# A fixed matmul order for the attention stage of a fused attention and two-layer-expert kernel

## The chip, the core and the metric

The kernel runs on one core of one Trainium2 chip. The metric is the device time of one execution in microseconds (us). Before the change three executions took 887.31, 887.38 and 888.92 us, median 887.38 us. The execution that the profiler recorded took 888.05 us.

## The reference

Three parts follow one another; the output of each is the input of the next.

```python
scores = scale * np.matmul(q, k.transpose(0, 1, 3, 2)) - np.log(S)   # q, k, v: 4 x 12 x 448 x 64
attn = 1.0 / (1.0 + np.exp(-scores))
x = np.matmul(attn, v)                                               # 48 heads
...
h = np.maximum(np.maximum(x @ w1, x @ w2), x @ w3)                   # 1792 x 768, weights 768 x 768
x = h @ w_out
...
h = x @ w_in                                                         # 768 x 2048
g = h * (1.0 / (1.0 + np.exp(-1.702 * h)))
out = g @ w_out
```

The attention weights come from a sigmoid and not from a softmax, so each block of scores can be weighed as soon as its own sigmoid is done. This case is about the first part.

## The kernel before

**The planner.** The program does not issue instructions while it describes the work. Every step is an `Op` with the engine or engines that can do it, an estimated length, a function that issues its instructions, and the memory it reads and writes. `Order.op` derives from the memory which earlier steps an `Op` must come after. `Order.run` then walks a simulated time and, for each engine, takes the ready step with the earliest due time (`late`). So the order of each engine's instructions is fixed when the program is built, and is the planner's. On the chip each engine runs its own list in order and waits on semaphores. For steps of TensorE, `Order.pe` keeps a running clock of the estimated lengths and gives every step that clock as its due time; another step's due time is worked back from those that need its result.

**The attention stage.** The 48 heads are worked on as 24 couples of two heads (`Couple`), and the couples in 12 cycles of two: x (even) and y (odd). The 448 keys of a head are 3 blocks of 128 and a last one of 64. For a couple there are these steps on TensorE:

- `score(c)`, line 581, for c = 0, 1, 2: scores of 128 keys against 448 queries. Queries and keys are split into a high and a low part, so three products of each head are summed: 6 matmuls, contraction 64, output 128 rows. The two heads lie in the two halves of the rows of TensorE's array. The result takes a pair of PSUM banks. There are three such pairs, used in turn.
- `score_last`, line 625: the last 64 keys of both couples of a cycle at once, four 64 by 64 matmuls in fp32.
- `weigh(c)`, line 599: the values times the sigmoids of a block, contraction 128, output 64 rows for each head: 2 matmuls in fp32, summed in a bank of the couple's own (6 for x, 7 for y).
- `weigh_last`, line 636: the same for the last 64 keys of both couples, four 64 by 64 matmuls.

The profile records an fp32 matmul as two instructions: a `weigh` is x4, `weigh_last` and `score_last` are x8, a `score` is x6. The three steps use the array in three shapes, which the profile writes as 64*128 (scores), 128*64 (weighing) and 64*64 (the last keys).

ScalarE takes each `score` from PSUM through a sigmoid (line 608), which also frees the pair of banks. ScalarE or VectorE copies a couple's finished bank out (line 307). The queries and keys of a couple are loaded (`in_qk`), split on VectorE with or without ScalarE (lines 307 and 310) into one of two slots, and the values are loaded (`in_vv`) into one of three slots. Beside that, `convert` prepares weights of the next stage, which come as 64-bit numbers: a load of 768 KB (`in_wa`), one instruction on ScalarE (line 355), four on VectorE (lines 365 to 370) and a store (`yk<-f`), two of these in each of cycles 1 to 9. All DMAs are issued by SyncE from one queue (SP), in order.

**The order before.** The loop lists, for cycle i: scores of x; the three `weigh` of the former y; `weigh_last` of the former cycle; `score_last`; scores of y; the three `weigh` of x. The listing only gives due times. The planner takes whichever ready step of TensorE is due first, and it moved `weigh` steps in between the scores.

Of the kernel before, what the change touches and what calls it, by code (L numbers as in the profile page):

```python
# [17 lines left out]
B, H, S, D = 4, 12, 448, 64  # L18
# [4 lines left out]
NPAIR = H // 2  # L23
# [4 lines left out]
HK = KC // 2  # L28
# [14 lines left out]
MM, FULL = 0.201, 0.752  # L43
# [44 lines left out]
class Order:  # L88


    def __init__(self):
        self.ops, self.clock = [], 0.0

    def op(self, on, fn, reads=(), writes=(), after=(), at=None, lag=None):
        lag = (LAND if "SP" in on else 0.1) if lag is None else lag
# [21 lines left out]
        return o  # L117

    def pe(self, fn, took, reads=(), writes=(), after=()):
        o = self.op({"PE": took}, fn, reads, writes, after, self.clock, 0.25)  # L120
        self.clock += took
        return o

    def run(self):
# [60 lines left out]
T = S  # L185
# [18 lines left out]
def moe_chain_kernel(tc, qk, vv, wa, wb, out):  # L204
    nc = tc.nc
    act, dve, pe, sp = nc.scalar, nc.vector, nc.tensor, nc.sync
    scale = 1.0 / math.sqrt(D)
    O = Order()
# [13 lines left out]
    psum = pspool.tile([P, 8, 512], F32, name="ps")  # L222
# [22 lines left out]
    def F(at, n):  # L245
        if at >= FAR2:
            return Reg(sn4, at - FAR2, n, lambda: slab_n[3][:, at - FAR2 : at - FAR2 + n])
        if at >= FAR:
            return Reg(sn1, at - FAR, n, lambda: slab_n[0][:, at - FAR : at - FAR + n])
        return Reg(sf, at, n, lambda: slab_f[:, at : at + n])  # L250
# [52 lines left out]
    def copy(to, of, n, psum=False, both=True):  # L303
        engines = {"ACT": t_act(n)}
        if both:
            engines["DVE"] = t_two(n) if psum else t_one(n)
        return O.op(engines, lambda e: (act.copy if e == "ACT" else dve.tensor_copy)(to(), of()), [of], [to])  # L307
# [15 lines left out]
    XA, XB = 0, FAR  # L323
# [223 lines left out]
    class Couple:  # L547
# [42 lines left out]
            self.a[c] = sigmoid(self.sc[c])  # L590

        def weigh(self, c):
            ps, v = self.av, self.v

            def f(_):
                w, o, x = v().rearrange("p (c d) -> p c d", d=D), ps(), self.a[c]()
                for e in range(2):
                    r = slice(e * D, (e + 1) * D)
                    pe.matmul(o[r], w[:, 2 * c + e], x[:, e * S : (e + 1) * S], start=c == 0, stop=False)  # L599

            O.pe(f, FULL + (0 if c else 0.15), [v, self.a[c]] + ([ps] if c else []), [ps])

    def sigmoid(ps):
        a = M1(a_at(), 2 * S)
        on(
            "ACT",
            t_act(2 * S) + 0.07,
            lambda: act.activation(  # L608
                a().rearrange("p (e s) -> p e s", e=2), ps(), AF.Sigmoid, bias=bias, scale=scale
            ),  # L610
            [ps],
            [a],
        )
        return a

    def score_last(two):

        ps = banks(d_at(), 2)

        def f(_):  # L620
            o = ps()
            for c, x in enumerate(two):
                for e in range(2):
                    r, t = slice(e * D, (e + 1) * D), x.t()
                    pe.matmul(o[c * D : (c + 1) * D, e, :], t[r, QK:QT], t[r, Q:QK], start=True, stop=True)

        O.pe(f, FULL, [x.t for x in two], [ps])
        return ps

    def weigh_last(two, a):  # L630
        def f(_):
            x = a()
            for c, y in enumerate(two):
                w, o, k = y.v().rearrange("p (c d) -> p c d", d=D), y.av(), slice(c * D, (c + 1) * D)
                for e in range(2):
                    pe.matmul(
                        o[e * D : (e + 1) * D], w[k, 6 + e], x[k, e * S : (e + 1) * S], start=False, stop=True
                    )

        O.pe(f, FULL + 0.15, [a, *(y.v for y in two), *(y.av for y in two)], [y.av for y in two])  # L640
        for y in two:
            b, hp = divmod(y.p, NPAIR)
            half, j = divmod(hp, HK)
            copy(F((XA if b < 2 else XB) + (6 * half + 3 * (b % 2) + j) * T, S), y.av, S, psum=True)

# [29 lines left out]
    prev, last = None, None  # L677
    for i in range(NP // 2):
        x = Couple(2 * i)
        x.values()  # L680
        if i == 0:
            x.score(0, slice(0, 1))
            x.score(1, slice(0, 1))
            x.score(0, slice(1, 3))
            x.scored(0)
            x.score(1, slice(1, 3))
            x.scored(1)
        for n in range(0 if i else 2, 3):
            x.score(n)
            x.scored(n)  # L690
        convert(x)
        for n in range(3 if prev else 0):
            prev[1].weigh(n)
        if prev:
            weigh_last(prev, last)
        y = Couple(2 * i + 1)
        y.values()
        last = sigmoid(score_last((x, y)))
        for n in range(3):
            y.score(n)  # L700
            y.scored(n)
        convert(y)
        for n in range(3):
            x.weigh(n)
        prev = (x, y)
    for n in range(3):
        prev[1].weigh(n)
    weigh_last(prev, last)
    gate["m"] = O.op({"-": 0.0}, to_m2, after=set(s1.ops))

    def pairs(base, half, tok, k):
# [48 lines left out]
    x = moving(XA)  # L760
# [3 lines left out]
    x = moving(XB)  # L764
    extra = []
    for fp in range(EARLY):
        for n in range(2):
            extra.append(lambda fp=fp, n=n: prepare(12 + fp, n, "ACT"))
        if fp < READY:
            w = []  # L770
# [99 lines left out]
    half = PAIRS // 2  # L870
# [144 lines left out]
    for n in range(7):  # L1015
# [22 lines left out]
        w = operand4(w)  # L1038
# [85 lines left out]
```

## Time and profile before

| | before |
|---|---|
| median of 3 runs | 887.38 us |
| the profiled execution | 888.05 us |
| its span, first to last instruction | 886.0 us |
| TensorE matmuls busy | 872.7 us (98%) |
| VectorE busy | 685.2 us (77%) |
| ScalarE busy | 504.2 us (57%) |
| DMA queue's packets, share of 16 engines | 75.7% |
| granted TensorE clock | 1.00 throughout, the upper of its two levels (2.4 GHz) |

The profiled execution is 2.05 us longer than its span, which lies around the span and is the same for both kernels. A matmul's recorded length overlaps the next one's, so lengths of steps on TensorE are read here from one group's start to the next group's start.

### The profile page before, as it was taken

How to read it: one execution, taken by the hardware profiler on the slowest of the kernel's cores; microseconds unless marked ns; L12 is line 12 of the kernel's file. 1: busy time of each engine (PE TensorE's matmuls, PEld its weight loads, DVE VectorE, ACT ScalarE, POOL GpSimd, SP SyncE). 2: the span in 40 equal slices, each digit the busy share in tenths (PEclk: the TensorE clock that was granted, in tenths of full speed). 3: DMA queues.
4: the chain of work that ended last, by engine and by line, in shares of the span. 5: the costliest groups of instructions: out<-in, count | busy, mean ns of one | idle time of the engine just before them, and what ended most of it. 6: DMA issues, size and time to landing. Idle time of an engine off the chain costs nothing.

```text
span 886.0 us, 12594 instructions
## 1 busy us (share of the span) xinstructions
PE 872.7 (98%) x4558; PEld 743.6 (84%) x4558; DVE 685.2 (77%) x1100; ACT 504.2 (57%) x738; POOL 1.1 (0%) x6
## 2 busy tenths in 40 slices
PE   9999999999999999999999999999999999999998
PEld 5444447999988987999988999999999999999997
DVE  5787878888899876778598888655778878863894
ACT  6888788455575745567476444556664544423540
POOL 0000000000000000000000000000000000000000
PEclk9999999999999999999999999999999999999999
DMA  7898977676749989879998965999867775686113
GB/s 271 287 343 287 318 275 238 209 251 240 280 196 337 394 285 359 257 260 319 355 410 329 383 212 154 376 367 334 302 244 282 267 258 153 203 286 209 32 63 125
DMA packets 77533, 238.13 MB, mean 269 GB/s; under 512 B 8608, under 2 KB 18208, under 8 KB 77472
## 3 DMA queue, kind: packets, MB, share of 16 engines
q1 hardware_dynamic: 77472, 237.34, 75.7%
q8 instruction: 36, 0.59, 0.3%
q14 instruction: 25, 0.20, 0.1%
HBM read 151.19 MB, written 86.11 MB: 268 GB/s over the span
## 4 chain that ended last, share of the span: by engine, by line
PE 64%; DVE 5%; DMA 3%; ACT 1%; issue 0%; DVEq 0%; SPq 0%; ACTq 0%
PE ps L490 38%; PE ps L851 7%; PE ps L850 7%; PE ps L852 7%; PE ps L992 6%; DVE f L310 2%; DMA r<-kept 2%; DVE r L310 2%; DMA kept<-r 1%; DMA yk<-f 1%; DVE m L310 0%; ACT f L360 0%; DVE f L370 0%; ACT r L307 0%; DVE n L310 0%
## 5 line engine op out<-in xcount | busy, mean ns | idle before, releaser
L490 PE MATMUL ps<-r 128*128 128x448 f32 x2250 | 466.8, 363 | 5.6 <-DVE f L310 2.4
L490 PEld LDWEIGHTS ps<-r 128*128 128x128 f32 x2250 | 421.1, 188 | 38.3 <-DVE r L310 2.2
L310 DVE TENSOR_TENSOR f<-ps,f 128x448 f32<-128x448 f32 x214 | 132.4, 622 | 88.3 <-PE ps L852 35.5
L310 DVE TENSOR_TENSOR r<-f,r 128x384 fp32r<-128x384 f32 (+3 forms) x252 | 160.2, 659 | 14.9 <-ACT r L307 14.2
L307 ACT CAST r<-f 128x384 fp32r<-128x384 f32 (+3 forms) x206 | 111.7, 571 | 65.5 <-PE ps L490 27.0
L307 ACT COPY f<-ps 128x448 f32<-128x448 f32 x130 | 69.7, 542 | 109.5 <-PE ps L490 71.5
L310 DVE TENSOR_TENSOR f<-f 128x384 f32<-128x384 f32 (+2 forms) x189 | 121.1, 658 | 7.6 <-ACT f L913 4.1
L608 ACT ACTIVATE m<-ps,bias 128x896 f32<-128x896 f32 x84 | 80.3, 1009 | 11.7 <-PE ps L581 10.5
L360 ACT ACTIVATE f<-f 128x768 uint8<-128x768 uint32 x38 | 74.9, 1970 | 0.6
L581 PEld LDWEIGHTS ps<-r 64*128 64x128 f32 x432 | 37.2, 185 | 34.2 <-ACT m L608 24.5
L355 ACT ACTIVATE f<-f 128x768 f32<-128x768 f32 x56 | 50.8, 910 | 23.6 <-DMA f<-in_wb 11.7
L599 PE MATMUL ps<-m,f 128*64 128x448 f32 x288 | 63.8, 555 | 0.0
L490 PE MATMUL ps<-m,r 128*128 128x448 f32 x270 | 58.9, 364 | 1.5 <-DVE r L307 0.7
L370 DVE SCALAR_TENSOR_TENSOR f<-f 128x768 uint32<-128x768 uint32 x56 | 53.2, 954 | 5.2 <-ACT f L360 4.6
L581 PE MATMUL ps<-r 64*128 64x448 f32 x432 | 56.4, 385 | 0.3 <-ACT m L608 0.2
L490 PEld LDWEIGHTS ps<-m,r 128*128 128x128 f32 x270 | 50.2, 188 | 6.6 <-DVE r L310 1.3
L365 DVE TENSOR_SCALAR f<-f 128x768 f32<-128x768 f32 x56 | 31.1, 555 | 18.5 <-ACT f L355 18.5
L307 ACT COPY ps<-ps 128x448 f32<-128x448 f32 x43 | 23.3, 542 | 34.9 <-PE ps L490 31.8
L307 ACT CAST m<-f 128x448 fp32r<-128x448 f32 (+4 forms) x36 | 26.1, 724 | 24.4 <-DVE f L310 16.4
L310 DVE TENSOR_TENSOR n<-f,n 128x448 fp32r<-128x448 f32 (+4 forms) x51 | 37.9, 745 | 2.0 <-ACT n L307 1.4
L599 PEld LDWEIGHTS ps<-m,f 128*64 128x64 f32 x288 | 16.7, 135 | 26.4 <-issue 22.8
L310 DVE TENSOR_TENSOR m<-f,m 128x448 fp32r<-128x448 f32 (+4 forms) x41 | 33.9, 831 | 4.0 <-ACT m L307 4.0
(81 smaller groups left out, 892.6 us busy)
## 6 DMA issues: line engine op xcount, KB each, us to landing
r<-kept SPq DMA_DIRECT2D x119, 384.0 KB, 5.2
kept<-r SPq DMA_DIRECT2D x112, 384.0 KB, 5.0
f<-in_wb SPq DMA_DIRECT2D x32, 768.0 KB, 7.2
f<-in_wa SPq DMA_DIRECT2D x24, 768.0 KB, 7.3
f<-yk SPq DMA_DIRECT2D x24, 768.0 KB, 6.0
yk<-f SPq DMA_DIRECT2D x40, 384.0 KB, 7.4
f<-y SPq DMA_DIRECT2D x24, 384.0 KB, 5.2
f<-in_qk SPq DMA_DIRECT2D x15, 456.0 KB, 5.8
```

The costliest lines, as they stand in the source:

```text
L307: return O.op(engines, lambda e: (act.copy if e == "ACT" else dve.tensor_copy)(to(), of()), [of], [to])
L310: return on("DVE", t_two(n), lambda: dve.tensor_tensor(to(), a(), b(), op=op), [a, b], [to])
L360: act.activation(byte(), words(raw(), U32, 0), AF.Copy, scale=LOW)
L370: lambda: dve.scalar_tensor_tensor(u(), words(raw(), U32, 1), 0x80000007, u(), **by),
L490: pe.matmul(o, a[:, c], b, start=fresh and j == n == 0, stop=j == HK - 1 and n == 2, skip_group_check=True,)
L581: pe.matmul(o[:, e, :], kx[r, c * P : (c + 1) * P], qx[r, Q:QK], start=n == 0, stop=n == 2)
L599: pe.matmul(o[r], w[:, 2 * c + e], x[:, e * S : (e + 1) * S], start=c == 0, stop=False)
L608: lambda: act.activation(a().rearrange("p (e s) -> p e s", e=2), ps(), AF.Sigmoid, bias=bias, scale=scale),
L850: pe.matmul(ps(), wh[:, c], gh, start=fresh and j == 0, **how)
L851: pe.matmul(ps(), wh[:, c], gl, start=False, **how)
L852: pe.matmul(ps(), wl[:, c], gh, start=False, stop=j == 1, skip_group_check=True)
L992: pe.matmul(o, a, b, start=fresh and k == n == 0, stop=k == 3 and n == 2, skip_group_check=True)
```

## The change

Every step of TensorE in the attention stage now also comes after the step listed before it (`self.row` in `Order.pe`), so the listed order is the order of TensorE; after the stage this is switched off. The listed order is changed: `weigh_last` of the former cycle and `score_last` follow the scores of x, and the three `weigh` of the former y come after them. `weigh_last` thereby becomes the first addend of y's bank and stays the last of x's, and y's bank is copied out (`give`) after its third `weigh` instead of after `weigh_last`.

```diff
@@ Order
-        self.ops, self.clock = [], 0.0
+        self.ops, self.clock, self.rows, self.row = [], 0.0, True, []
...
     def pe(self, fn, took, reads=(), writes=(), after=()):
-        o = self.op({"PE": took}, fn, reads, writes, after, self.clock, 0.25)
+        o = self.op({"PE": took}, fn, reads, writes, [*after, *self.row], self.clock, 0.25)
         self.clock += took
+        if self.rows:
+            self.row = [o]
         return o
@@ Couple.weigh
-            ps, v = self.av, self.v
+            ps, v, second = self.av, self.v, self.p % 2 == 1
+            begin, end = c == 0 and not second, c == 2 and second
...
-                    pe.matmul(o[r], w[:, 2 * c + e], x[:, e * S : (e + 1) * S], start=c == 0, stop=False)
-
-            O.pe(f, FULL + (0 if c else 0.15), [v, self.a[c]] + ([ps] if c else []), [ps])
+                    pe.matmul(o[r], w[:, 2 * c + e], x[:, e * S : (e + 1) * S], start=begin, stop=end)
+
+            O.pe(f, FULL + (0 if c else 0.15), [v, self.a[c]] + ([] if begin else [ps]), [ps])
+            if end:
+                self.give()
@@ weigh_last
-                        o[e * D : (e + 1) * D], w[k, 6 + e], x[k, e * S : (e + 1) * S], start=False, stop=True
+                        o[e * D : (e + 1) * D], w[k, 6 + e], x[k, e * S : (e + 1) * S], start=c == 1, stop=c == 0
...
-        for y in two:
...
-            copy(F((XA if b < 2 else XB) + (6 * half + 3 * (b % 2) + j) * T, S), y.av, S, psum=True)
+        two[0].give()
@@ the loop over cycles
         convert(x)
-        for n in range(3 if prev else 0):
-            prev[1].weigh(n)
         if prev:
             weigh_last(prev, last)
         y = Couple(2 * i + 1)
         y.values()
         last = sigmoid(score_last((x, y)))
+        for n in range(3 if prev else 0):
+            prev[1].weigh(n)
         for n in range(3):
             y.score(n)
...
+    weigh_last(prev, last)
     for n in range(3):
         prev[1].weigh(n)
-    weigh_last(prev, last)
+    O.rows, O.row = False, []
```

The new lines move the line numbers: scores 581 to 583, `weigh` 599 to 602, the sigmoid 608 to 618, `score_last` 625 to 635, `weigh_last` 636 to 646, the next stage's matmul 490 to 492.

TensorE, one cycle before (581 scores, 599 weighing, 636 `weigh_last`, 625 `score_last`):

```order
L581 MATMUL ps<-r 128x448 x12
L599 MATMUL ps<-m_76,f 64x448 x2
L581 MATMUL ps<-r 128x448 x6
L599 MATMUL ps<-m_76,f 64x448 x4
L581 MATMUL ps<-r 128x448 x12
L599 MATMUL ps<-m_76,f 64x448 x2
L581 MATMUL ps<-r 128x448 x6
L599 MATMUL ps<-m_76,f 64x448 x4
L636 MATMUL ps<-m_76,f 64x448 x4
L625 MATMUL ps<-f 64x448 x4
```

and one cycle now (583 scores, 602 weighing, 646 `weigh_last`, 635 `score_last`):

```order
L583 MATMUL ps<-r 128x448 x18
L646 MATMUL ps<-m_76,f 64x448 x4
L635 MATMUL ps<-f 64x448 x4
L602 MATMUL ps<-m_76,f 64x448 x6
L583 MATMUL ps<-r 128x448 x18
L602 MATMUL ps<-m_76,f 64x448 x6
```

The same matmuls stand in two unbroken groups of scores and two of weighing, where there were four of each.

SyncE's queue, the loads of one cycle before (with what each waits for):

```order
L298 DMA f<-in_vv 128x512 [waits DMAHW3_49,PE_49]
L298 DMA f<-in_vv 128x512 [waits DMAHW4_49,PE_49]
L298 DMA n_77<-in_qk 128x912 [waits DMAHW5_49,PE_49]
L298 DMA f<-in_qk 128x912 [waits DMAHW6_49,DVE_49,PE_49]
L351 DMA f<-in_wa 128x768 [waits DMAHW7_49,DVE_49,Activation_49]
L292 DMA yk_436<-f 128x768 [waits DMAHW0_49]
```

and now:

```order
L300 DMA f<-in_vv 128x512 [waits DMAHW3_49,PE_49]
L300 DMA n_77<-in_qk 128x912 [waits DMAHW4_49,PE_49]
L300 DMA f<-in_qk 128x912 [waits DMAHW5_49,DVE_49,PE_49]
L300 DMA f<-in_vv 128x512 [waits DMAHW6_49,PE_49]
L353 DMA f<-in_wa 128x768 [waits DMAHW7_49,DVE_49,Activation_49]
L294 DMA yk_445<-f 128x768 [waits DMAHW0_49]
```

One of the two loads of values moved behind the loads of queries and keys; nothing else in the cycle's queue did.

SyncE's queue at the start of the program, before (the first couple's queries and keys come in three pieces, 512, 256 and 144 wide):

```order
L298 DMA f<-in_qk 128x512
L298 DMA f<-in_qk 128x256
L298 DMA f<-in_qk 128x144
L298 DMA f<-in_qk 128x912
L298 DMA f<-in_vv 128x512
```

and now:

```order
L300 DMA f<-in_qk 128x512
L300 DMA f<-in_qk 128x256
L300 DMA f<-in_qk 128x912
L300 DMA f<-in_qk 128x144
L300 DMA f<-in_vv 128x512
```

The second couple's load of 456 KB moved ahead of the first couple's third piece of 72 KB.

## Rows read from the trace of the kernel before

**Rows 1.** Waits of TensorE, 0 to 135 us: us in total, times, longest.
```profile
PE ps L581 <- ACT m L608: 0.2, 1, 0.2
```

**Rows 2.** Windows of 10 us: busy us per engine, clock, DMA share, GB/s.
```profile
50.00:60.00 10.00, 10.00 (x72) 4.49 (x70) 9.69 (x15) 7.92 (x11) 0.00 (x0) 1.00 0.99 350
...
260.00:270.00 10.00, 8.84 (x41) 7.52 (x42) 10.00 (x17) 5.18 (x11) 0.00 (x0) 1.00 0.55 219
...
320.00:330.00 10.00, 8.46 (x42) 7.59 (x41) 8.10 (x17) 6.46 (x11) 0.00 (x0) 1.00 0.93 317
...
340.00:350.00 10.00, 9.01 (x44) 7.86 (x43) 6.05 (x12) 6.87 (x7) 0.00 (x0) 1.00 1.02 414
```

**Rows 3.** Timeline of TensorE, one cycle: start us, length us, engine, line, shape.
```profile
64.78 1.48 PE L581 MATMUL ps<-r 64*128 64x448 f32 x12
66.19 0.97 PE L599 MATMUL ps<-m,f 128*64 128x448 f32 x4
67.09 0.87 PE L581 MATMUL ps<-r 64*128 64x448 f32 x6
67.89 1.72 PE L599 MATMUL ps<-m,f 128*64 128x448 f32 x8
69.55 1.49 PE L581 MATMUL ps<-r 64*128 64x448 f32 x12
...
74.33 0.98 PE L636 MATMUL ps<-m,f 64*64 64x448 f32 x8
75.13 0.93 PE L625 MATMUL ps<-f 64*64 64x448 f32 x8
75.99 1.48 PE L581 MATMUL ps<-r 64*128 64x448 f32 x12
```

**Rows 4.** Timeline of TensorE, start and end of the attention stage.
```profile
5.42 2.08 PE L581 MATMUL ps<-r 64*128 64x448 f32 x18
7.43 0.98 PE L625 MATMUL ps<-f 64*64 64x448 f32 x8
8.65 2.67 PE L581 MATMUL ps<-r 64*128 64x448 f32 x18 [0.24 <-ACT m L608]
11.35 2.48 PE L599 MATMUL ps<-m,f 128*64 128x448 f32 x12
13.76 1.48 PE L581 MATMUL ps<-r 64*128 64x448 f32 x12
...
24.70 1.48 PE L581 MATMUL ps<-r 64*128 64x448 f32 x12
...
125.61 1.49 PE L581 MATMUL ps<-r 64*128 64x448 f32 x12
...
139.99 0.47 PE L490 MATMUL ps<-r 128*128 128x448 f32 x1
```

**Rows 5.** Timeline of ScalarE, first pieces of queries and keys.
```profile
5.33 0.31 ACT L307 CAST r<-f 128x144 fp32r<-128x144 f32 x1 [1.31 <-DMA f<-in_qk]
6.79 0.90 ACT L307 CAST r<-f 128x848 fp32r<-128x848 f32 x1 [1.15 <-DMA f<-in_qk]
```

**Rows 6.** DMA issues from 20 to 130 us: KB each, median us to landing.
```profile
f<-in_wa SPq DMA_DIRECT2D x15, 768.0 KB, 8.1
yk<-f SPq DMA_DIRECT2D x17, 384.0 KB, 7.6
f<-in_qk SPq DMA_DIRECT2D x12, 456.0 KB, 6.2
f<-in_vv SPq DMA_DIRECT2D x19, 256.0 KB, 3.2
```

**Rows 7.** Timeline of ScalarE in the cycle of rows 3.
```profile
65.00 2.81 ACT L608 ACTIVATE m<-ps,bias 128x896 f32<-128x896 f32 x3
68.07 1.01 ACT L608 ACTIVATE m<-ps,bias 128x896 f32<-128x896 f32 x1 [0.26 <-PE ps L581]
68.97 0.90 ACT L355 ACTIVATE f<-f 128x768 f32<-128x768 f32 x1
```

More of the change, by code (lines that the diff above doesn't have):

```diff
@@ L598, in f, with give @@
                     r = slice(e * D, (e + 1) * D)
-                    pe.matmul(o[r], w[:, 2 * c + e], x[:, e * S : (e + 1) * S], start=c == 0, stop=False)
-            O.pe(f, FULL + (0 if c else 0.15), [v, self.a[c]] + ([ps] if c else []), [ps])
+                    pe.matmul(o[r], w[:, 2 * c + e], x[:, e * S : (e + 1) * S], start=begin, stop=end)
+            O.pe(f, FULL + (0 if c else 0.15), [v, self.a[c]] + ([] if begin else [ps]), [ps])
+            if end:
+                self.give()
+        def give(self):
+            b, hp = divmod(self.p, NPAIR)
+            half, j = divmod(hp, HK)
+            copy(F((XA if b < 2 else XB) + (6 * half + 3 * (b % 2) + j) * T, S), self.av, S, psum=True)
     def sigmoid(ps):
@@ L636, in f @@
                     pe.matmul(
-                        o[e * D : (e + 1) * D], w[k, 6 + e], x[k, e * S : (e + 1) * S], start=False, stop=True
+                        o[e * D : (e + 1) * D], w[k, 6 + e], x[k, e * S : (e + 1) * S], start=c == 1, stop=c == 0
                     )
-        O.pe(f, FULL + 0.15, [a, *(y.v for y in two), *(y.av for y in two)], [y.av for y in two])
-        for y in two:
-            b, hp = divmod(y.p, NPAIR)
-            half, j = divmod(hp, HK)
-            copy(F((XA if b < 2 else XB) + (6 * half + 3 * (b % 2) + j) * T, S), y.av, S, psum=True)
+        O.pe(f, FULL + 0.15, [a, two[0].av, *(y.v for y in two)], [y.av for y in two])
+        two[0].give()
     warm = R(0, 2 * T)
```

## The prediction

> **What bounds the kernel now.** I read the waits of TensorE first, then the windows, then TensorE's timeline through one cycle.
>
> In the attention stage TensorE waits once, for 0.2 us, after its warm-up matmuls [rows 1]. A window inside the stage shows it busy 10.00 of 10 us, while VectorE at 9.69 us and the DMAs at a share of 0.99 are nearly full as well [rows 2]. So the stage lasts as long as TensorE's own work, and a wait removed elsewhere would bring nothing; the other engines have little room left.
>
> The timeline shows that this work is not only matmuls [rows 3]. From start to start, 12 score matmuls take 66.19 - 64.78 = 1.41 us and 6 take 67.89 - 67.09 = 0.80 us. One block of scores is therefore 0.61 us, and 0.20 us are paid once per group, whatever its size. A `weigh` of 4 takes 67.09 - 66.19 = 0.90 us and 8 take 69.55 - 67.89 = 1.66 us: 0.76 us each and 0.15 us once per group. Each time the array's shape changes, the stream loses 0.15 to 0.20 us. Here it also holds for long groups: 18 scores take 7.43 - 5.42 = 2.01 us = 3 x 0.605 + 0.20, and 12 `weigh` matmuls 13.76 - 11.35 = 2.41 us = 3 x 0.755 + 0.15 [rows 4].
>
> Behind attention TensorE is short of work only in places, in the windows at 260, 320 and 340 us [rows 2]; over the whole span it idles 886.0 - 872.7 = 13.3 us.
>
> **The change, part by part.**
>
> *Fewer groups.* A cycle before is 75.99 - 64.78 = 11.21 us [rows 3], and from cycle 2 to cycle 10 each is as long: (125.61 - 24.70) / 9 = 11.21 us [rows 4]. A cycle now is scores of x (2.01), `weigh_last` (75.13 - 74.33 = 0.80), `score_last` (75.99 - 75.13 = 0.86), three `weigh` (2.41), scores of y (2.01), three `weigh` (2.41): 10.50 us. One passage of it the trace does not have: `score_last` followed by `weigh`. Before, scores followed, at 0.86 us. From below I bound it by 0.80, a 64*64 group followed by one of its own shape; from above by 0.76 + 0.20 = 0.96, a group with the dearest change of shape. I take 0.86, the same group with another change of shape behind it. A cycle then lasts 10.44 to 10.60 us and saves 0.71 us (0.61 to 0.77).
>
> *Eleven cycles and the tail.* Cycle 1 begins at 13.76 us, and the next stage's first matmul at 139.99 us [rows 4]. Now: 13.76 + 11 x 10.50 = 129.26 us, then `weigh_last` alone (0.86, a change of shape behind it) and the last three `weigh` (2.41): 132.53 us. The saving is 139.99 - 132.53 = **7.46 us**, 6.3 to 8.1 us with the bounds above taken eleven times.
>
> *The start.* The load of 456 KB moves ahead of the piece of 72 KB. Before, the small piece had landed by 5.33 us and the large one by 6.79 us [rows 5]; exchanged, the small piece is late by up to 6.79 - 5.33 = 1.46 us, and the large one some 0.2 us early. The third block of scores needs the small piece and would have started at about 5.42 + 1.41 = 6.83 us. Cast and subtraction of that piece take about 0.3 us each, which would put it at 7.1 to 7.4 us: 0.3 to 0.6 us late. Against that, ScalarE is through with the large piece's cast earlier, begins the sigmoids earlier, and y's first scores, which stretched to 11.35 - 8.65 = 2.70 us instead of 2.01 behind those sigmoids [rows 4], gain up to 0.7 us. I take 0, with -0.6 to +0.6.
>
> *The planner's new answer for the other engines.* The sigmoids, splits, copies and prepares are the same in number and must fit into 10.50 us. One load of values moves behind the loads of queries and keys. The slot it waits for is set free by `weigh_last`, now 2.81 us into the cycle, or by the former y's weighing; what is loaded is used a cycle later, against 3.2 us to landing [rows 6]. Nothing. The third couple's queries after next wait for `score_last` (now 3.7 us into the cycle) and are next used 10.50 + 2.81 = 13.3 us into it: 9.6 us, against 6.2 us to landing [rows 6]. Nothing, as long as the queue isn't longer by 3.4 us. The copies out of PSUM are the same; y's bank is used again 6.4 us after its last `weigh`. Nothing.
>
> *ScalarE behind three blocks of scores in a row.* A sigmoid starts 0.98 us after its scores (68.07 - 67.09) and takes 0.90 us (68.97 - 68.07) [rows 3, 7]. `score_last` takes the first block's pair of banks, 2.81 us into the cycle, and that pair is free at 1.9 us: 0.9 us to spare. Nothing, unless two more instructions of ScalarE stand in between.
>
> The Trainium skill speaks against the change here: "TensorEngine Tiling (Array Packing)", Performance Considerations, says that packing speeds up TensorE but not the reading out of PSUM, which may become the limit. By that rule a cycle would last as long as ScalarE's part. The window shows 7.92 of 10 us of it [rows 2], 8.9 us of a cycle of 11.21: the trace puts that limit below 10.50 us.
>
> *Sum.* Behind the stage everything starts 7.46 us earlier, and I let the whole of it arrive at the end, since no later wait is for something that happens at a fixed time. 888.05 - 7.46 = 880.6 us for the profiled execution; the median of the runs lies 0.67 us below that execution, so **880.0 us**.
>
> **The rivals.**
>
> *A. The DMAs bound the nine cycles with two prepares.* Such a cycle moves 2 x (456 + 256 + 768 + 384) KB [rows 6] = 3.82 MB, which is 340 GB/s over 11.21 us and 364 over 10.50. In the fullest window 350 GB/s took a share of 0.99 [rows 2]. At 350 a cycle lasts 10.91 us, nine of them give back 3.7 us, and the time is 883.7 us. For it: no room in that window. Against it: only queries, keys and values, 1.46 MB, are due within the cycle, and the prepares can slip into the cycles 10 and 11 and further; a later window moved 414 GB/s [rows 2].
>
> The Trainium skill, "DMA: Bandwidth & Descriptors", Specifications, gives about 358 GB/s as the limit of one core's share of HBM. By it such a cycle would take 10.7 us, and the change would lose 1.5 us of its gain. The 414 GB/s of the later window disagree.
>
> *B. Slower: `score_last` waits for the sigmoid.* The order is now rigid: if `score_last`'s pair of banks isn't free, TensorE stands, where before it took a `weigh` first. With two instructions of 0.90 us [rows 7] ahead of the cycle's first sigmoid, started when that could have started, the wait is 1.8 - 0.9 = 0.9 us. In eleven cycles that is 9.9 us, more than the 7.46 saved: 889.8 us. It decides from a delay of 0.9 + 7.46 / 11 = 1.6 us per cycle. For it: blocks of scores come every 0.61 us and sigmoids take 0.90; the stretched 2.70 us at 8.65 us is just this wait [rows 4]. Against it: the second half of the cycle has three sigmoids in 4.4 us, so ScalarE can do the other two before the cycle begins.
>
> *C. Nothing arrives.* In the windows at 260 and 320 us VectorE is full, or TensorE short, while loads and stores run [rows 2]. If these places wait for a chain of VectorE and DMA work that does not start with TensorE's progress, they swallow the gain: 887.4 us. Against it: VectorE is busy for 77% of the span only, and most of its work in the next stage is on TensorE's results.
>
> *D. More arrives.* The planner charges a change of shape only once per three blocks, so with its own extra groups it ran some 7 us ahead of the chip by the end of the stage. Now its times fit, and of the 13.3 us that TensorE idles some 3 may go: 877 us.
>
> That the change does not do what it says is excluded by the instruction order.
>
> **How the numbers follow.** Forecast 0.66, A 0.14, B 0.06, C 0.07, D 0.07. The forecast's own range is 878.8 to 881.8 us from the bounds of the missing passage and the start. The range of 8 in 10 takes in A, and D to its middle: 877.5 to 884.3 us. A measurement of this kernel can tell about 0.2% (1.8 us) from no change: the forecast, A and D are faster by more (0.87), C is within it (0.07), B is slower (0.06).
>
> **What would show each step.** Right: a cycle of 10.4 to 10.6 us from scores of x to scores of x, groups of x18 and x12, no wait of TensorE in the stage over 0.5 us, and the next stage's first matmul at 131.9 to 133.7 us. A would show as waits of VectorE's casts for `in_qk`, with TensorE waiting behind them. B would show as waits of `score_last` (line 635) for ScalarE. C would show as a first matmul at 132.5 us and the window at 250 to 270 us with more idle TensorE than now. The prediction is wrong if the cost per group is not of the change of shape but of something that the larger groups keep, such as waiting for weights to load: then 12 and 18 in a row would show gaps inside the group.

## The result, and the profile after

Four executions of the changed kernel took 876.97 to 879.87 us, median **878.68 us**, against 887.38 us: a ratio of 0.9896 [0.9877, 0.9916]. The forecast was 880.0 us with a range of 877.5 to 884.3 us. The profiled execution took 878.68 us, 9.37 us less than the one of before. Three pieces make up that difference: TensorE's first matmul of the next stage starts 139.99 - 133.49 = 6.50 us earlier, the span from there to its end is 3.0 us shorter (876.5 - 133.49 = 743.0, before 886.0 - 139.99 = 746.0), and what lies around the span is 0.13 us longer.

The page's busy times after. VectorE is 4.8 us busier than before and ScalarE 1.2 us less; TensorE is busy 8.2 us less, with the same matmuls:

```profile
PE 864.5 (99%) x4558; PEld 747.7 (85%) x4558; DVE 690.0 (79%) x1107; ACT 503.0 (57%) x731; POOL 1.1 (0%) x6
```

TensorE's timeline after (start us, length us, engine, line, shape, in brackets a wait and its releaser), to be read beside [rows 3]:

```profile
34.78 2.08 PE L583 MATMUL ps<-r 64*128 64x448 f32 x18
36.79 0.98 PE L646 MATMUL ps<-m,f 64*64 64x448 f32 x8
37.59 0.93 PE L635 MATMUL ps<-f 64*64 64x448 f32 x8
38.45 2.48 PE L602 MATMUL ps<-m,f 128*64 128x448 f32 x12
40.86 2.08 PE L583 MATMUL ps<-r 64*128 64x448 f32 x18
42.87 2.48 PE L602 MATMUL ps<-m,f 128*64 128x448 f32 x12
45.28 1.08 PE L583 MATMUL ps<-r 64*128 64x448 f32 x8
...
87.28 2.08 PE L583 MATMUL ps<-r 64*128 64x448 f32 x18
89.29 0.98 PE L646 MATMUL ps<-m,f 64*64 64x448 f32 x8
90.93 0.59 PE L635 MATMUL ps<-f 64*64 64x448 f32 x2 [0.66 <-ACT m L618]
...
98.67 2.08 PE L583 MATMUL ps<-r 64*128 64x448 f32 x18
...
133.49 6.68 PE L492 MATMUL ps<-r 128*128 128x448 f32 x32
```

A cycle is 45.28 - 34.78 = 10.50 us, the forecast to the hundredth, and ten of the eleven last that long. The passage that the trace of before lacked, `score_last` into weighing, is 38.45 - 37.59 = 0.86 us. One cycle lasts 98.67 - 87.28 = 11.39 us: `score_last` waits for ScalarE. What ScalarE and VectorE did then, in the timeline of the same kernel:

```profile
86.53 0.91 ACT L357 ACTIVATE f<-f 128x768 f32<-128x768 f32 x1
...
87.94 1.04 DVE L364 TENSOR_SCALAR f<-f 128x768 uint16<-128x768 uint16 x1
89.07 0.90 ACT L309 CAST r<-n 128x848 fp32r<-128x848 f32 x1 [1.64 <-DVE f L364]
...
89.88 2.80 ACT L618 ACTIVATE m<-ps,bias 128x896 f32<-128x896 f32 x3
```

ScalarE stood idle for 1.64 us in front of a cast of queries and keys, and the three sigmoids behind it in its list stood with it. The first began at 89.88; 0.98 us after its scores it could have begun at 88.26. That is 1.62 us late; less the 0.9 us to spare of the prediction it is 0.7 us, and TensorE waited 0.66. The profile names VectorE's line 364 as the releaser, which ended at 88.98. But that instruction works on a tile (`f`) that the cast does not touch. The cast also waits for its load. SyncE's issue of it, and its landing in the DMA view of 78 to 92 us:

```profile
81.10 0.38 SPq L300 DMA_DIRECT2D n<-in_qk  x1
...
n<-in_qk SPq DMA_DIRECT2D x1, 456.0 KB, 7.9
```

81.10 + 7.9 = 89.0 us. I take the load as what was late; the two ended within 0.1 us of each other, so this trace alone does not settle it. Two kernels of the experiments do, *the last prepare late* and *all of them late*. Up to 128 us their ScalarE, VectorE and DMA queue run the same instructions in the same order as here. In the first this load took 5.4 us to land, the cast did not wait, and the cycle lasted 10.50 us. In the second it took 7.7 us, the cycle lasted 10.87 us, and the profile names the load as what the cast waited for:

```profile
88.23 0.90 ACT L309 CAST r<-n 128x848 fp32r<-128x848 f32 x1 [1.12 <-DMA n<-in_qk]
```

So the stall comes from the time that one load takes to land, which differs from execution to execution under the same order. The windows show how full the DMAs were after (busy us of PE, PEld, DVE, ACT, POOL; clock, DMA share, GB/s):

```profile
50.00:60.00 10.00, 10.00 (x76) 5.02 (x74) 8.86 (x14) 8.41 (x11) 0.00 (x0) 1.00 0.92 344
90.00:100.00 10.00, 9.34 (x68) 4.64 (x66) 9.41 (x14) 8.88 (x11) 0.00 (x0) 1.00 1.02 386
```

The window that holds the late steps has the highest DMA share and rate of the stage, 386 GB/s, and more work of ScalarE than the one at 50 us.

**The other 3.0 us** lie behind attention. From the next stage's first matmul to the run of 36 matmuls behind the passage from layer 1 to layer 2 it is 264.30 - 133.49 = 130.8 us, before 273.33 - 139.99 = 133.3: 2.5 us less. This time is called the passage below. To a run of 72 near 450 us another 0.7 us go, and the rest gives back 0.2. TensorE's matmuls behind attention are the same in both traces, in the same order. TensorE's waits at 240 to 280 us (waiter, releaser; total us, times, longest), before:

```profile
PE ps L490 <- DVE r L310: 1.4, 3, 0.5
PE ps L490 <- DVE f L310: 0.8, 1, 0.8
```

and after:

```profile
PE ps L492 <- DVE f L312: 0.8, 1, 0.8
```

The three waits for VectorE's splits of the next layer's input are gone. VectorE's timeline says what had changed there. Line 370 (372 after) is the last of a `prepare`'s four instructions on VectorE. Before:

```profile
243.95 0.96 DVE L370 SCALAR_TENSOR_TENSOR f<-f 128x768 uint32<-128x768 uint32 x1
244.83 0.62 DVE L310 TENSOR_TENSOR f<-ps,f 128x448 f32<-128x448 f32 x1
...
258.18 2.08 DVE L310 TENSOR_TENSOR r<-f,r 128x896 fp32r<-128x896 f32 x3
```

and after:

```profile
230.62 0.96 DVE L372 SCALAR_TENSOR_TENSOR f<-f 128x768 uint32<-128x768 uint32 x1
...
241.80 1.16 DVE L312 TENSOR_TENSOR f<-ps,f 128x448 f32<-128x448 f32 x2 [0.30 <-PE ps L492]
```

Before, this last instruction of the stage's last prepare began 104.0 us into the stage (243.95 - 139.99), and from 242 us to the end of the passage VectorE had no gap: it was behind, and TensorE waited for it. After, it begins 97.1 us into the stage (230.62 - 133.49), and up to 244 us VectorE still has gaps in which it waits for TensorE. The start of this instruction, counted from the stage's start, is called the place of the last prepare below. So the planner dealt the prepares of layer 1 otherwise, although the change touches only attention's order.

### The profile page after: what moved, and what is told of

It is laid out like the page before. It is cut to its first block, busy times and chain, and to the rows that moved or that the text cites. A ratio compares the mean times of both kernels' runs of the same rounds, so it can differ in the third digit from the quotient of the medians.

```text
span 876.5 us, 12583 instructions
## 1 busy us (share of the span) xinstructions
PE 864.5 (99%) x4558; PEld 747.7 (85%) x4558; DVE 690.0 (79%) x1107; ACT 503.0 (57%) x731; POOL 1.1 (0%) x6
## 4 chain that ended last, share of the span: by engine, by line
PE 94%; DVE 4%; DMA 1%; ACT 1%; issue 1%; POOLq 0%; DVEq 0%; POOL 0%; ACTq 0%
PE ps L492 53%; PE ps L859 7%; PE ps L858 7%; PE ps L860 7%; PE ps L602 7%; PE ps L1000 6%; PE ps L583 6%; DVE f L312 2%; DVE r L312 1%; PE ps L646 1%; PE ps L635 1%; DMA kept<-r 1%; PE ps L662 0%; DVE m L312 0%; ACT r L309 0%
## 5 line engine op out<-in xcount | busy, mean ns | idle before, releaser
L312 DVE TENSOR_TENSOR f<-ps,f 128x448 f32<-128x448 f32 x214 | 132.5, 623 | 90.8 <-PE ps L860 35.4
L309 ACT CAST r<-f 128x384 fp32r<-128x384 f32 (+3 forms) x206 | 113.7, 580 | 66.0 <-PE ps L492 30.5
L309 ACT COPY f<-ps 128x448 f32<-128x448 f32 x124 | 66.5, 540 | 109.5 <-PE ps L492 75.8
L602 PE MATMUL ps<-m,f 128*64 128x448 f32 x288 | 59.4, 548 | 0.0
L583 PEld LDWEIGHTS ps<-r 64*128 64x128 f32 x432 | 39.3, 187 | 19.1 <-ACT m L618 9.2
L583 PE MATMUL ps<-r 64*128 64x448 f32 x432 | 50.7, 376 | 0.0
L602 PEld LDWEIGHTS ps<-m,f 128*64 128x64 f32 x288 | 18.5, 136 | 34.4 <-issue 31.7
```

The costliest lines, as they stand in the source:

```text
L312: return on("DVE", t_two(n), lambda: dve.tensor_tensor(to(), a(), b(), op=op), [a, b], [to])
L583: pe.matmul(o[:, e, :], kx[r, c * P : (c + 1) * P], qx[r, Q:QK], start=n == 0, stop=n == 2)
```

## The experiments

Two theories stood against each other for attention. *Groups*: the time went because the shape of the array changes less often. *Order*: it went because the last keys' steps moved. For the 3.0 us behind it they were *prepare* (the last prepares end earlier), *fits* (rival D: the planner's times now fit the chip) and *chance* (any new dealing moves the later stages by this much).

**The old list, fixed.** The kernel of before, with the new rule that the listed order is TensorE's order, and nothing else. This gives groups of 18 and 12 without the move.

```diff
...
-        o = self.op({"PE": took}, fn, reads, writes, after, self.clock, 0.25)
+        o = self.op({"PE": took}, fn, reads, writes, [*after, *self.row], self.clock, 0.25)
         self.clock += took
+        if self.rows:
+            self.row = [o]
...
+    O.rows, O.row = False, []
```

> The fixing alone: the listing of the kernel before, each step of TensorE held behind the one listed before it. TensorE then runs two groups of 18 scores and two of 12 weighing matmuls per cycle, as in the change, but the last keys' steps stand where they stood. Theory (the gain is the number of groups, 0.15 to 0.20 us each): a cycle of 2.01 + 2.41 + 0.80 + 0.86 + 2.01 + 2.41 = 10.5 us, the next stage's first matmul at 131.9 to 133.7 us, and 878 to 881 us. Rival (the gain comes from moving the last keys' steps ahead of the weighing, which lets loads start earlier): a cycle stays near 11.2 us and the time near 887 us.

Measured: 881.33 us, 0.9938 [0.9915, 0.9961]. Cycles without a wait last 24.34 - 13.75 = 10.59 us, so the groups alone bring the cycle down. The forecast of the stage missed: in the profiled execution, the slowest of four (885.43 us; the others 880.82 to 881.51), the first matmul of the next stage starts at 141.31 us, 1.3 us later than in the kernel before. TensorE's waits up to 140 us:

```profile
PE ps L583 <- ACT m L610: 5.0, 4, 2.1
```

and TensorE's timeline where the longest of them lies:

```profile
74.19 1.48 PE L583 MATMUL ps<-r 64*128 64x448 f32 x12
77.75 0.88 PE L583 MATMUL ps<-r 64*128 64x448 f32 x6 [2.08 <-ACT m L610]
78.56 4.17 PE L601 MATMUL ps<-m,f 128*64 128x448 f32 x12
```

In the old list the scores of y follow `score_last` at once, so y's third block needs a pair of banks that ScalarE has not yet read; in the new list 2.41 us of weighing lie between. ScalarE's timeline shows what stood in front of the sigmoids here:

```profile
75.08 0.89 ACT L357 ACTIVATE f<-f 128x768 f32<-128x768 f32 x1 [2.21 <-DMA yk<-f]
75.87 0.93 ACT L309 CAST r<-f 128x896 fp32r<-128x896 f32 x1
76.70 2.80 ACT L610 ACTIVATE m<-ps,bias 128x896 f32<-128x896 f32 x3
```

a prepare's instruction that waited 2.21 us for a store to leave its buffer. So the groups shorten the cycle, and I read the move as cover for ScalarE. The two kernels differ by 881.33 - 878.68 = 2.65 us by the medians; how much of that is attention, the profile of the slowest execution does not tell. What that execution gained on the kernel before, 2.6 us, lies behind attention, which it ended late: 883.5 - 141.31 = 742.2 us, against 746.0.

**The new list, free.** The changed kernel with the rule switched off from the start; only the listing and its due times remain.

```diff
-        self.ops, self.clock, self.rows, self.row = [], 0.0, True, []
+        self.ops, self.clock, self.rows, self.row = [], 0.0, False, []
```

> The listing alone: the change's listing and its new start and end of each bank's sum, but the planner is free to move TensorE's steps. Its instruction order shows the same groups of 18 and 12 as the change. Theory (groups): a cycle of 10.5 us and a first matmul of the next stage at 132 to 134 us, as with the change; so listing and fixing would each do it alone. Rival (the fixed order itself matters, through the due times of the other engines): the groups are there and the stage is still longer by over 2 us.

Measured: 881.31 us, 0.993 [0.9915, 0.9945]. TensorE's groups are the same, ten of its eleven cycles last 10.50 us, and the next stage begins at 133.89 us, 0.4 us later than in the change. The listing alone makes the groups whole. But the span behind that point is 745.3 us, and TensorE's waits at 240 to 280 us are those of before:

```profile
PE ps L492 <- DVE r L312: 1.4, 3, 0.5
PE ps L492 <- DVE f L312: 0.8, 1, 0.8
```

The place of the last prepare is 104.1 us, and the passage takes 133.4. So the 3.0 us do not come with the shorter attention, nor with TensorE's order there, but with how the planner dealt the other engines' work. *Fits* falls: the planner's times fit as well here.

**Twelve groups.** The list of before, fixed, with one `weigh` after each block of scores.

```diff
             x.scored(n)
+            if prev:
+                prev[1].weigh(n)
         convert(x)
-        for n in range(3 if prev else 0):
-            prev[1].weigh(n)
...
             y.scored(n)
+            x.weigh(n)
         convert(y)
-        for n in range(3):
-            x.weigh(n)
...
```

> More groups: the listing of the kernel before, fixed, with one block of weighing behind each block of scores, so six groups of 6 scores and six of 4 weighing matmuls per cycle instead of two and two. All matmuls, sigmoids and loads are the same. Theory (each further group of scores with its group of weighing costs 0.20 + 0.15 us): a cycle of 10.50 + 4 x 0.35 = 11.9 us, the next stage's first matmul some 15 us later than with the change, at 147 to 149 us, and 892 to 895 us. Rival (TensorE's time per cycle is set by waits for sigmoids or banks, which spaced scores would relax): a cycle at or below 11.2 us, at most 887 us.

Measured: 895.87 us, 1.0089 [1.0072, 1.0106]. TensorE's timeline:

```profile
68.42 0.88 PE L583 MATMUL ps<-r 64*128 64x448 f32 x6
69.23 0.97 PE L601 MATMUL ps<-m,f 128*64 128x448 f32 x4
...
80.33 0.88 PE L583 MATMUL ps<-r 64*128 64x448 f32 x6
```

The cycle is 80.33 - 68.42 = 11.91 us. The prices of the prediction give 10.50 + 4 x (0.20 + 0.15) = 11.90 for four more pairs of groups. The next stage begins at 148.16 us, inside the forecast; the time lies above the 892 to 895 us expected, because the span behind attention is 893.8 - 148.16 = 745.6 us, without the change's 3.0. With the same matmuls, the number of groups sets the time: *groups* holds in both directions.

**The charge corrected.** The kernel of before, with the planner charging a change of shape at the places where its own grouping makes one.

```diff
-            O.pe(f, (some.stop - some.start) * MM + (0 if c else 0.21), reads, [ps])
+            O.pe(f, (some.stop - some.start) * MM + (0.21 if c in (0, 2) else 0), reads, [ps])
...
-            O.pe(f, FULL + (0 if c else 0.15), [v, self.a[c]] + ([ps] if c else []), [ps])
+            O.pe(f, FULL + (0.15 if c in (0, 1) else 0), [v, self.a[c]] + ([ps] if c else []), [ps])
```

> The kernel before with nothing changed but two of the planner's estimates: a change of shape is charged twice per three blocks instead of once. The planner, free as before, then puts scores in groups of 18 and weighing in groups of 12 in nearly all cycles. Theory (groups): cycles of 10.5 us where the groups are whole, a first matmul of the next stage at 132 to 135 us, 878 to 882 us. On the second gain, 2.5 us in the passage from the first to the second layer: if it came from a plan whose times fit the chip, it is here as well; if it came from the new listing, the passage takes as long as in the kernel before.

Measured: 884.48 us, 0.9961 [0.9946, 0.9976], a miss. Groups were not whole in all cycles, and TensorE waited 2.0 us in four places for sigmoids; the next stage began at 137.12 us. Fitting times in the planner bring a third of the change, 2.9 of 8.7 us. The passage had no wait at all and took 129.7 us (place of the last prepare: 82.6 us). What it gained was lost again: at 300 to 500 us TensorE waited 6.5 us, before 5.5, and behind the longest of these waits, 2.13 us at 458 us, the granted clock fell (last section).

**One group of weighing.** The changed kernel, with the former y's weighing put behind the scores of y, so that six `weigh` follow each other and one pair of shape changes goes.

```diff
         last = sigmoid(score_last((x, y)))
-        for n in range(3 if prev else 0):
-            prev[1].weigh(n)
         for n in range(3):
             y.score(n)
+        for n in range(3):
+            if prev:
+                prev[1].weigh(n)
             y.scored(n)
```

> One step further: the former y's three weighing steps move behind the scores of y, so a cycle is scores of x, both last-key steps, scores of y, and one group of 24 weighing matmuls; y's sigmoids are listed behind the weighing that frees their memory. Theory (groups): a cycle of 2.01 + 0.80 + 0.86 + 2.01 + 6 x 0.755 + 0.15 = 10.36 us, 0.14 less than with the change, the next stage's first matmul at 131 us, 877 us. Rival (ScalarE: seven sigmoids now follow scores that come in 5.7 us, and y's must wait for the weighing): TensorE waits for sigmoids by over 0.2 us per cycle, and the time is 879 us or more.

Measured: 878.57 us, 0.9895 [0.9879, 0.9912], the same as the change, where 877 us and a cycle of 10.36 us were expected. TensorE's timeline:

```profile
13.69 2.08 PE L583 MATMUL ps<-r 64*128 64x448 f32 x18
...
17.37 2.17 PE L583 MATMUL ps<-r 64*128 64x448 f32 x18
19.47 4.73 PE L602 MATMUL ps<-m,f 128*64 128x448 f32 x24
24.13 1.08 PE L583 MATMUL ps<-r 64*128 64x448 f32 x8
```

The cycle is 10.44 us: the weighing is shorter, but y's scores take 19.47 - 17.37 = 2.10 us instead of 2.01. I read that as a pair of banks that comes free late, since they follow `score_last` at once as in the old list, where they take 2.10 us as well. One cycle, with a wait of 0.52 us for a sigmoid, lasts 11.68 us. Taking one more pair of shape changes out of TensorE's order brought nothing here.

**The casts on VectorE.** The changed kernel, with the casts of queries and keys of all but the first two couples bound to VectorE. ScalarE's list then holds no step that waits for `in_qk`.

```diff
-                copy(hp, tp, n)
+                if p < 2:
+                    copy(hp, tp, n)
+                else:
+                    on("DVE", t_one(n), lambda hp=hp, tp=tp: dve.tensor_copy(hp(), tp()), [tp], [hp])
```

> The change, with the casts of queries and keys on VectorE alone from the third couple on, so ScalarE's queue never holds an instruction that waits for their load. In the change one cycle of eleven took 11.4 us: the step of the last 64 keys waited 0.66 us for a sigmoid, which stood behind such a cast on ScalarE, and the cast waited for its load. Theory: that wait goes, eleven cycles of 10.5 us, the next stage's first matmul at 132.6 us instead of 133.5, some 0.9 us less in all if the later stages are dealt alike. Rival (the load itself was late, and the scores of that couple would wait in any case; or VectorE with six more casts falls behind): a wait of the same size appears at the scores instead, no gain.

Measured: 879.82 us, 0.991 [0.9894, 0.9925]. TensorE has no wait for a sigmoid in the whole stage and the next one begins at 131.69 us, 1.8 us earlier than in the change. Half of that lies in the start: cycle 1 begins at 12.87 us, though up to there both kernels run the same instructions in the same order. The other half is the missing stall, and that does not show what the cast's move is worth, for the stall is also missing in *the last prepare late*, where the cast stands as in the change. Nothing of it reaches the end: the place of the last prepare is 102.5 us, the passage took 133.3 us again, and around 330 us the granted clock fell (last section).

**The planner's landing time.** The kernel of before, dealt anew by a small change of one estimate.

```diff
-LAND, LAND_RAW = 1.0, 2.0
+LAND, LAND_RAW = 1.1, 2.0
```

> The kernel before with one of the planner's estimates changed that belongs to no engine's work (the time a DMA takes to land, 1.0 to 1.1). It measures how far the time moves when the planner deals the same work in another way. If the later stages are sensitive to that, the time from the attention stage's end to the end moves by 1 us or more against the kernel before, in either direction; if not, by less than 0.5 us. The attention stage itself should keep its groups and stay within 0.5 us of 140.0 us.

Measured: 887.69 us over ten executions, 1.0005 [0.9994, 1.0017]. The next stage begins at 141.03 us, 0.5 us outside the forecast. The span behind attention is 745.6 us and the passage 133.3 us, with the last prepare at 102.7 us. A new dealing does not by itself move the later stages by 3 us; one case is no proof against *chance*, but it speaks against it for the 2.5 us of the passage. For the 0.7 us near 450 us it speaks the other way: from the run of 36 to the run of 72 this kernel takes 181.1 us, as the change does (445.47 - 264.30 = 181.2), and the kernel before 455.22 - 273.33 = 181.9.

**The last prepare late.** The changed kernel, with the sixth of layer 1's prepares held back behind TensorE's steps.

```diff
...
+                i // 2, i % 2, "ACT", XA + 12 * T, [o for o in O.ops if "PE" in o.on][-1:] if i == 23 else ()
...
```

> The change, with the load of the last of the six weight prepares of layer 1 held behind the product that TensorE runs when the program comes to it, about 94 us after that stage's start. In the kernel before that load was issued 94.9 us after the stage's start, with the change 87.3. Theory (of the gain beyond attention, 2.5 us come from VectorE being through with the last prepare before its full stretch at the passage to layer 2): TensorE waits there 2 to 3 us longer than with the change, 880 to 882 us. Rival (that gain has another cause, such as where the splits and sums stand in VectorE's order): the passage takes as long as with the change, within 0.5 us.

Measured: 878.3 us, 0.9891 [0.9876, 0.9906]. The place of the last prepare is 105.6 us, and the passage took 131.87 us, 1.06 us more than in the change: the right direction, and 1.06 of the 2.5 us to explain. The time did not rise to the 880 to 882 us expected. Behind attention it took 744.3 us, 1.2 more than the change, but attention ended at 132.14 us in this execution, 1.35 us earlier, by an earlier start and without the stall.

**All of them late.** Two empty places ahead of the six prepares, and the first and the last of them held back.

```diff
...
+        [lambda: None] * 2
+        + [
...
+                i // 2, i % 2, "ACT", XA + 12 * T, [o for o in O.ops if "PE" in o.on][-4:-3] if i in (18, 23) else ()
...
```

> The change, with the first of layer 1's six prepares held back by some 22 us and the last one's load to some 93 us after the stage's start, so that all six run about as late as in the kernel before (there the last one's final instruction on VectorE came 104 us after the stage's start, with the change 97 us; holding back the last alone cost 1.1 us of 2.5 in the passage). Theory (the passage to layer 2 takes the longer, the later VectorE has done its share of prepares): 133.0 to 133.5 us from the stage's first matmul to the first run of 36 matmuls behind the passage, as before, instead of 130.8; 880 to 882 us. Rival (something else in the new deal): 131.9 us or less, as with the last alone.

Measured: 878.59 us, 0.9891 [0.9875, 0.9907], again below the 880 to 882 us expected. The place of the last prepare is 106.6 us, the passage 132.21 us: 1.4 of the 2.5 us. The span behind attention is 744.4 us, and attention ended at 132.64 us. *Prepare* holds for that much; 1.1 us stay open.

The other kernels, in which nothing was held back and no due time given, fall in line. Where the last prepare stands at 102.5 to 104.5 us, the passage takes 133.3 to 133.4 us (the kernel before, the new list free, twelve groups, the casts, the landing time); at 93.1 to 97.1 us it takes 130.1 to 130.8 (the change, the old list fixed, one group of weighing); at 82.6 us, 129.7 (the charge). That the two kernels with held prepares, at 105.6 and 106.6 us, stay below 132.3 us shows that this place alone does not set it.

**Due times for the prepares.** The changed kernel, with a due time every 13 us from the beginning of layer 1 for these six prepares, where before only the need for their results gave them one.

```diff
-    layer1(x, True, XA, [lambda i=i: prepare(i // 2, i % 2, "ACT", XA + 12 * T) for i in range(18, 24)])
+    def due(i):
+        n = len(O.ops)
+        prepare(i // 2, i % 2, "ACT", XA + 12 * T)
+        for o in O.ops[n:]:
+            o.at = begun + 13.0 * (i - 18)
+
+    begun = O.clock
+    layer1(x, True, XA, [lambda i=i: due(i) for i in range(18, 24)])
```

> The change with the second repair alone, the due times of layer 1's prepares. Theory: the attention stage as with the change (133.5 us, with one wait of TensorE for a sigmoid), and the passage without waits, 129.5 to 130.1 us instead of 130.8: about 0.8 us less than the change, 877.5 to 878.5 us. Rival (prepares ahead of their old time take VectorE from the splits of operands): waits of TensorE for VectorE within the stage's first 100 us.

Measured: 873.37 us (three executions at 873.03 to 873.5, one at 880.16), 0.9854 [0.9822, 0.9886], better than the 877.5 to 878.5 expected, but not in the way expected. The place of the last prepare is 60 us. The passage takes 132.5 us instead of the forecast 129.5 to 130.1, longer than in the change, because the rival came true early in the stage, where TensorE waits for VectorE:

```profile
132.17 11.08 PE L492 MATMUL ps<-r 128*128 128x448 f32 x54
145.00 2.05 PE L492 MATMUL ps<-r 128*128 128x448 f32 x9 [1.75 <-DVE f L312]
```

The windows of the passage to layer 2 and of the next one at 320 us, after the change:

```profile
240.00:260.00 20.00, 20.00 (x101) 18.51 (x100) 19.41 (x34) 13.68 (x25) 0.00 (x0) 1.00 0.33 130
260.00:280.00 20.00, 19.21 (x97) 17.71 (x96) 18.75 (x33) 12.62 (x25) 0.00 (x0) 1.00 0.97 366
320.00:340.00 20.00, 17.85 (x83) 15.14 (x84) 13.37 (x28) 8.78 (x13) 0.00 (x0) 1.00 1.01 405
```

and with due times:

```profile
240.00:260.00 20.00, 20.00 (x102) 18.74 (x101) 18.30 (x31) 14.83 (x28) 0.00 (x0) 1.00 0.41 160
260.00:280.00 20.00, 20.00 (x102) 18.75 (x101) 17.33 (x31) 11.72 (x23) 0.00 (x0) 1.00 1.03 386
320.00:340.00 20.00, 20.00 (x102) 18.75 (x101) 16.71 (x33) 8.50 (x13) 0.00 (x0) 1.00 1.01 385
```

TensorE is full in these windows, also in those at 320 us, which I had not expected; why it follows was not tried. The gain lies there: from the run of 36 to the run of 72 it takes 176.4 us, 4.8 less than the change. The span behind attention is 739.3 us, 3.8 less than in the change. Attention has no stall, and the next stage begins at 132.17 us, 1.3 us earlier; start and stall differ that much under the same order (see *the last prepare late*), so I do not put this down to the due times.

**Casts and due times; and the one group of weighing with both.** The edits above, together.

> The change with two repairs: casts of queries and keys on VectorE alone from the third couple on (no sigmoid behind a load), and layer 1's six prepares given due times 13 us apart from the stage's start. Theory: attention ends at 131.7 to 132.7 us, and VectorE has done the last prepare by some 80 us after that, so TensorE waits for nothing at the passage, as it did in the run with two changed charges: from the stage's first matmul to the run of 36 behind the passage 129.5 to 130.1 us instead of 130.8; 876 to 877.5 us. Rival (the later stages lose by the new deal what the passage gains): the time is 878 us or more though both repairs show.

Measured: 873.95 us, 0.9841 [0.9826, 0.9856], below the 876 to 877.5 expected; the passage, forecast at 129.5 to 130.1 us, takes 132.3, with the same wait of 1.75 us at 145 us. Next to due times alone the casts bring nothing.

> The same two repairs on the kernel with one group of 24 weighing matmuls per cycle. Its cycles took 10.44 us, 0.06 less than the change's, and one cycle in eleven waited for a sigmoid. Theory: that wait goes, attention ends 0.6 us before that of the kernel with two groups and the repairs, 875.5 to 877 us. Rival (y's third block of scores waits for the sigmoid of the last keys, now without weighing in between): cycles over 10.5 us, no gain over the kernel with two groups.

Measured: **872.37 us** (871.4 to 873.17), 0.9824 [0.9809, 0.9838], the fastest median of the study: 6.3 us below the change. The forecast was 875.5 to 877 us. Its attention ends no earlier than without the one group (132.70 against 132.56 us), so the 1.6 us that it is ahead of the version before it lie in later stages. The traces say where: the wait of 1.75 us at 145 us is not there, and the passage takes 129.7 us. Why the planner's answer avoids that wait was not tried. Its interval overlaps that of due times alone; which of the two is faster is not shown.

## Why the prediction was right, and where it was not

- *Fewer groups*: right. 10.50 us per cycle, 0.86 us from `score_last` into weighing, groups of 18 and 12 without gaps; twelve groups cost 1.41 us more, as the prices say. That the listed order also cures this without the rule was not foreseen.
- *Eleven cycles and the tail*: 132.53 us was predicted, 133.49 measured. 0.89 us of it is the one stall, 0.02 the start, 0.05 the tail.
- *The start, taken as 0*: 13.78 against 13.76 us. Both parts had the right sign: x's scores took 2.75 us instead of 2.01, more than the 0.3 to 0.6 us late that was worked out, and y's were back at 2.00 us. That they cancel to 0.02 us is luck: with the same order, cycle 1 began at 13.14 us in *the last prepare late* and at 13.46 in *all of them late*.
- *"Nothing, unless two more instructions of ScalarE stand in between"* is the step that failed, once in eleven cycles of this execution. The 0.9 us to spare was right; what used it up was one instruction that itself waited for a load. The step on the loads had asked only whether the scores get their data in time, not who is queued behind the cast on ScalarE. This is rival B's mechanism at a price of 0.89 us, once, instead of 9.9; with the same order and other landing times the price was 0 and 0.37 us. The old list, fixed, shows waits for sigmoids at 5.0 us, there at the scores of y.
- *Rival A* fell with its premise: 350 GB/s at a share of 0.99 was no ceiling. The DMAs moved 386 GB/s in the window at 90 us, and the nine cycles with two prepares show no common delay. The figure of about 358 GB/s in the Trainium skill ("DMA: Bandwidth & Descriptors", Specifications) is passed here as well.
- *Rival C* fell: the gain arrived, and TensorE's waits at 240 to 280 us fell from 2.2 to 0.8 us.
- *"I let the whole of it arrive"*: 3.0 us more arrived. That was rival D's size, but not its cause. The new list, free, has the same attention and not the 3.0 us, and the corrected charge alone brought 3 us in all. The step took it that what lies behind attention keeps its length; it did not ask what the planner would deal anew there. The cause that the runs support is the planner's new dealing of layer 1's last prepares, shown for 1.4 of the 2.5 us at the first passage; the 0.7 us near 450 us also stand in a kernel without the change (the landing time), and the rest is open.

The two misses, 0.96 us lost and 3.0 us gained, leave the predicted 880.6 us of the profiled execution 1.9 us too high (0.13 us lie outside the span). They have opposite signs, so the small error of the sum is in part luck. The forecast of the median is rounded up: 880.59 - 0.67 is 879.9, not 880.0.

## What to carry to other kernels

Count the groups between changes of the array's shape and price them from one timeline: that gave the cycle to 0.01 us. When matmuls are put in a fixed order, ask of each engine that frees their banks what may wait in its list ahead of that work, loads and stores above all. And where a planner deals the order, an edit in one stage deals the next one anew, so read the stages behind the edit as well. Background work without a due time of its own moved by 7 us here; with due times the kernel was 5.3 us faster by the medians, although the passage for which they were meant became longer. Before a stall of under 1 us is put down to an edit, compare executions that run the same order: start and stall together differed by 1.35 us between two of them.

## What the runs showed of the chip that was not expected

In the old list, fixed, TensorE stood for 2.08 us at 75.7 to 77.75 us. The windows behind it (columns as above):

```profile
78.00:80.00 2.00, 2.00 (x12) 0.90 (x12) 2.00 (x3) 2.00 (x3) 0.00 (x0) 0.74 1.04 413
80.00:82.00 2.00, 2.00 (x6) 0.51 (x6) 1.46 (x4) 2.00 (x3) 0.00 (x0) 0.50 1.04 357
82.00:84.00 2.00, 2.00 (x18) 1.25 (x16) 2.00 (x5) 0.36 (x2) 0.00 (x0) 0.91 1.01 358
```

The granted clock went from 1.00 to 0.50, the lower of the two levels (1.2 GHz), and 12 `weigh` matmuls took 82.66 - 78.56 = 4.10 us instead of 2.41. So that wait cost 1.7 us more than its length. With the charge corrected the clock also went to 0.50, at 460 to 462 us, behind a wait of 2.13 us. With the casts on VectorE it did so after waits of 1.43 us at 321 us and 1.30 us at 328 us:

```profile
330.00:332.00 2.00, 2.00 (x7) 1.79 (x6) 1.70 (x4) 0.39 (x1) 0.00 (x0) 0.50 1.04 428
```

In the changed kernel the waits at the same two places, 1.54 us at 320 us and 1.08 us at 327 us, left the clock at 1.00, and so did the wait of 1.75 us at 145 us with due times. What sets these apart was not tried.
